# Last transform stage in sets of four banks, first weights split by row blocks, and the last sums in another order, in a kernel that mixes a long convolution with a bilinear GLU

## The chip, the cores and the metric

One core of a Trainium2 chip runs the whole kernel. The time is the device time of one execution in microseconds (us); the kernel before has a median of 628.41 us over 3 runs (627.85 to 631.08). The engines are PE (matrix products, with PEld for its weight loads), DVE (VectorE), ACT (ScalarE), POOL (GpSimd, here a queue for DMAs that add in memory) and SP (a queue for all other DMAs).

## The reference

For 2048 tokens of 512 channels the output is a gated mix of two branches, `g * a + (1 - g) * b`, with `g = sigmoid(sum(x * gate_w))` for each token.

```python
def _A_ref(u, log_A_real, A_imag, C_real, C_imag, log_dt, D_skip):
    dt = jnp.exp(log_dt)
    A = -jnp.exp(log_A_real) + 1j * A_imag
    C = (C_real + 1j * C_imag) * dt[:, None]
    P = jnp.exp((A * dt[:, None])[:, :, None] * pos[None, None, :])
    K = 2.0 * jnp.einsum("dn,dnl->dl", C, P).real
    ...                       # a causal convolution of u with K by FFTs of 2 * L points
    return y + u * D_skip[None, None, :]
def _B_ref(x, w_gate, w_up, w_down):
    g = jnp.einsum("bsd,df->bsf", x, w_gate)
    u = jnp.einsum("bsd,df->bsf", x, w_up)
    return jnp.einsum("bsf,fd->bsd", g * u, w_down)
```

F, the inner width of the GLU, is 1792, and the state has 128 numbers for each channel.

## The kernel before

**The GLU branch** works through 14 blocks of 128 inner columns (f) in five groups of 3, 2, 3, 3 and 3, and in each group through four chunks of 512 tokens. To keep float32 accuracy every operand is split into a high part (rounded to float32r by an ACT cast: `xhi`, `whi`, `dhi`, `hh`) and a low part (what is left, by a DVE subtraction: `xlo`, `wlo`, `dlo`, `hl`), and every block product of 128 rows and 512 columns is three matmuls: high x low, low x high, high x high. For one f and one chunk, `hidden` makes 12 matmuls into the bank `pg` (gate) and 12 into `pu` (up); ACT copies `pg` to `h`, DVE multiplies `pu` into it, ACT and DVE split it to `hh` and `hl`. `down` then sums all f of the group into four `y` banks, of which two exist. ACT scales a finished `y` by 1 - g into `acc`, and a DMA stores it (first group, SP) or adds it to the output in memory (later groups, POOL). These 2016 matmuls, one by one, are called products below.

**The convolution branch** is done by Fourier transforms written as small matmuls. `u_part` takes 8 sets of first transforms of the input (`k<-in,w_t` in the trace) and stores them to the memory tensor `su_d`. For each of 16 blocks of 32 channels DVE and ACT build the tables `x` and `v` of powers, and one set of matmuls (`k<-v,x`, `k_block`) makes the kernel K from them. After every fourth block the quarter q of the channels is complete: `k_first` transforms its K in two sets (`k<-kt,w1k_t`, stored to `sk_d`), `m_second` makes four sets (`w2s`), `m_product` multiplies on DVE, `m_inverse` makes two sets back (`k<-y,w3s`, stored to `y_d`), and `m_last` the last stage (`w4`): it reads `y_d` back and makes two calls for each quarter, each of two banks; ACT multiplies them by the gate g into a staging tile `ts`, which POOL adds to the output. All these sets share four banks `k`. In the last quarter the tables are read into tiles that are free by then (`late`), the mixing is on DVE, and the part for tokens 12 to 15 of each partition stays in SBUF (`late["fin"]`).

**The end.** `ends` takes the output rows of the last chunk, as far as they were summed in memory, into the tile `kt` and for each of four row blocks adds the last `y` times 1 - g (`scalar_tensor_tensor`), then `late["fin"]` for the last 128 channels, and stores the block by SP.

**The start.** `first_loads` issues the first chunk's x, and the weights of f 0, 1 and 2, into tiles that are free at first. Three warm-up matmuls on zeros (each leaves two records) run meanwhile.

**The order of the work** is planned when the program is built. Each step is added as a task with its engine, an estimate of its time, what it reads and writes, a rank and sometimes an earliest time (`after`). `Work.run` places the tasks greedily: of all that could start, the one with the earliest start, then the lowest rank. The order that comes out is then the fixed program order of each engine. A `hidden` step n may not be planned before `T_STEP * n`, with `T_STEP = 10.3`. So an edit of one task's cost or start moves much of the order behind it.

## Time and profile before

| | |
|---|---|
| median of 3 runs | 628.41 us (627.85 to 631.08) |
| the profiled execution | 627.43 us, span 625.7 us |
| PE busy | 607.1 us, 97% of the span |
| DVE, ACT, POOL busy | 513.7, 421.7, 88.8 us |
| DMA | 121.67 MB, mean 194 GB/s |

The span runs from the first to the last record of the profile; the time of the execution is 1.7 us more. The profile gives, for groups of instructions or one by one, when they ran, how long, and what ended an engine's wait before them. Matmuls overlap, so a row's length is longer than its place in the sequence: products follow one another every 0.23 us, though each row says 0.39.

### The profile page before, as it was taken

To read this page: it belongs to the slowest core of one execution; us is meant where nothing else is said; L and a number is where in the kernel's file an instruction comes from. 1 tells how busy PE (TensorE), PEld (TensorE's weight loads), DVE (VectorE), ACT (ScalarE), POOL (GpSimd) and SP (SyncE) were. 2 spreads that over 40 slices of the span, in tenths; PEclk is the share of its full clock that TensorE was granted. 3 is DMA by queue.
4 is the path that set the end of the run, shared out by engine and by line. 5 is a ranking of instruction groups with operands and counts; after the bars stand their busy time and mean duration, and the time that the engine had idled before them with its cause. 6 is when DMAs were issued, how large, how long until landed. Compare 5 with 4: busy or idle time off the path is not lost.

```text
span 625.7 us, 17973 instructions
## 1 busy us (share of the span) xinstructions
PE 607.1 (97%) x7526; PEld 468.4 (75%) x7526; DVE 513.7 (82%) x808; ACT 421.7 (67%) x951; POOL 88.8 (14%) x125
## 2 busy tenths in 40 slices
PE   8999999999999899999999999999999999999993
PEld 5676777787678678877788887868788887777871
DVE  6959999999899989999749999989999962329543
ACT  6478878886895976697658866886977563534310
POOL 0211121111022101113101111030201020121101
PEclk9999999999999999999999999999999999999998
DMA  8793745555679994877667966793997959797866
GB/s 317 215 323 100 244 120 179 169 177 152 180 170 247 230 234 116 216 213 99 136 184 197 252 214 126 220 215 100 231 237 190 252 148 270 195 266 170 186 170 118
DMA packets 102422, 121.67 MB, mean 194 GB/s; under 512 B 6596, under 2 KB 65476, under 8 KB 102084
## 3 DMA queue, kind: packets, MB, share of 16 engines
q1 hardware_dynamic: 83188, 92.46, 48.1%
q0 software_dynamic: 19008, 28.06, 25.2%
q8 instruction: 59, 0.97, 0.6%
q14 instruction: 23, 0.19, 0.1%
q10 hardware_dynamic: 144, 0.00, 0.0%
HBM read 69.37 MB, written 51.12 MB: 193 GB/s over the span
## 4 chain that ended last, share of the span: by engine, by line
PE 79%; DVE 6%; DMA 5%; issue 5%; ACT 3%; SPq 0%; ACTq 0%; DVEq 0%; POOLq 0%
PE y L100 21%; PE pu L100 20%; PE pg L100 20%; PE k L100 18%; DMA out<-acc 2%; DMA raw<-in_wts 2%; DVE v L100 1%; DMA in<-in_u 1%; DVE x L100 1%; DMA ev<-in_wts 1%; DVE h L100 1%; DVE hl L100 1%; DVE wlo L100 1%; ACT acc L100 1%; DVE xlo L100 0%
## 5 line engine op out<-in xcount | busy, mean ns | idle before, releaser
L100 POOL DMA_DIRECT2D out<-acc x60 | 53.2, 943 | 351.3 <-ACT acc L100 337.8
L100 PE MATMUL y<-dhi,hl 128*128 128x512 f32 x224 | 91.5, 408 | 2.8 <-issue 1.8
L100 PE MATMUL pg<-xhi,wlo 128*128 128x512 f32 x224 | 89.6, 400 | 2.0 <-DVE wlo L100 1.0
L100 PE MATMUL pu<-xhi,wlo 128*128 128x512 f32 x224 | 89.3, 399 | 0.0
L100 PE MATMUL pg<-xlo,whi 128*128 128x512 f32 x224 | 87.5, 391 | 1.2 <-issue 0.9
L100 PE MATMUL y<-dlo,hh 128*128 128x512 f32 x224 | 87.5, 391 | 0.0
L100 PE MATMUL y<-dhi,hh 128*128 128x512 f32 x224 | 87.4, 390 | 0.0
L100 PE MATMUL pg<-xhi,whi 128*128 128x512 f32 x224 | 87.3, 390 | 0.0
L100 PE MATMUL pu<-xlo,whi 128*128 128x512 f32 x224 | 87.3, 390 | 0.0
L100 PE MATMUL pu<-xhi,whi 128*128 128x512 f32 x224 | 87.3, 390 | 0.0
L100 DVE TENSOR_TENSOR h<-pu,h 128x512 f32<-128x512 f32 x56 | 38.6, 689 | 51.5 <-PE pu L100 42.7
L100 ACT ACTIVATE acc<-y,ngate 128x512 f32<-128x512 f32 x76 | 51.5, 693 | 29.0 <-PE y L100 20.0
L100 ACT CAST hh<-h 128x512 fp32r<-128x512 f32 x56 | 34.7, 620 | 47.0 <-DVE h L100 46.8
L100 PEld LDWEIGHTS y<-dhi,hl 128*128 128x128 f32 x224 | 42.0, 187 | 25.4 <-issue 10.4
L100 ACT COPY ts<-k 128x512 f32<-128x512 f32 (+1 forms) x116 | 49.3, 496 | 14.2 <-PE k L100 14.2
L100 PEld LDWEIGHTS pg<-xhi,wlo 128*128 128x128 f32 x224 | 42.0, 188 | 17.2 <-issue 2.3
L100 ACT COPY h<-pg 128x512 f32<-128x512 f32 x56 | 32.9, 587 | 30.5 <-PE pg L100 24.9
L100 PEld LDWEIGHTS pu<-xhi,wlo 128*128 128x128 f32 x224 | 42.0, 188 | 13.5 <-issue 4.2
L100 PEld LDWEIGHTS pg<-xlo,whi 128*128 128x128 f32 x224 | 42.1, 188 | 10.2 <-issue 1.3
L100 PEld LDWEIGHTS y<-dhi,hh 128*128 128x128 f32 x224 | 42.1, 188 | 9.3
L100 PEld LDWEIGHTS pu<-xhi,whi 128*128 128x128 f32 x224 | 42.0, 188 | 9.0
L100 PEld LDWEIGHTS pg<-xhi,whi 128*128 128x128 f32 x224 | 42.1, 188 | 8.9
(103 smaller groups left out, 1169.3 us busy)
## 6 DMA issues: line engine op xcount, KB each, us to landing
raw<-in_xT SPq DMA_DIRECT2D x60, 256.0 KB, 4.4
out<-acc POOLq DMA_DIRECT2D x60, 256.0 KB, 7.0
raw<-in_wts SPq DMA_DIRECT2D x36, 256.0 KB, 5.4
su_d<-ts POOLq DMA_DIRECT2D x32, 256.0 KB, 4.7
sk_d<-ts SPq DMA_DIRECT2D x16, 512.0 KB, 5.2
y_d<-ts SPq DMA_DIRECT2D x16, 512.0 KB, 5.3
in<-sk_d SPq DMA_DIRECT2D x12, 512.0 KB, 6.8
in<-su_d SPq DMA_DIRECT2D x12, 512.0 KB, 5.9
```

The costliest lines, as they stand in the source:

```text
L100: got = getattr(self.engine, name)(*args, **kw)
```

## The change

Four edits:

1. `m_last` takes a list of halves. For quarters 0 to 2 it is now one call of eight matmuls over all four `k` banks (`halves = (0, 1)`), with four reads of `y_d` before it, of which the fourth goes to a `y` tile; for the last quarter it stays two calls of two banks. In `k_first`, the last quarter's second half is staged in two table tiles (`ri`, `e`).
2. The weights of f 0 come in four DMAs, each with the 128 columns of gate and of up that belong to one row block kt, alternating with the four DMAs of x; the first of them is issued by ACT. `first_split` splits each piece by itself (256 columns). The first `hidden` uses the high x high matmul first and high x low last. One warm-up matmul of the three is dropped.
3. The earliest time of every `hidden` is 5.0 us earlier.
4. In `ends` the addition of `late["fin"]` comes before that of `y`.

```diff
@@ -401,12 +401,15 @@
         in_y = lambda shape: new("mid", "y", shape, bufs=2)
         in_ev = lambda shape: new("mid", "ev", shape, bufs=3)
         xsrc = lambda kt: xT[P * kt : P * kt + P, :D]
-        w0 = load_two(lambda k: ("w", 0, k), in_ev, None, False)
-        x01 = load_two(lambda k: ("x", 0, 0, k), in_y, None, False)
-        for t, k, src in ((x01, 0, xsrc(0)), (w0, 0, wts[0][:, :D]), (w0, 1, wts[0][:, D : 2 * D]), (x01, 1, xsrc(1))):
-            add("sp", 0.42, lambda t=t, k=k, src=src: sp.dma_start(t.t[:, k], src), w=[(t, k)], dma=256, rank=-1)
-        x23 = xT[2 * P : 4 * P, :D].rearrange("(k p) t -> p k t", k=2)
-        load_two(lambda k: ("x", 0, 0, 2 + k), in_y, x23)
+        w0 = raws["w0"] = in_ev([P, 2, D])
+        xt = [load_two(lambda k, n=n: ("x", 0, 0, 2 * n + k), in_y, None, False) for n in range(2)]
+        wsrc = wts[0][:, : 2 * D].rearrange("p (k d) -> p k d", k=2)
+        for kt in range(KT):
+            t, k, ks = xt[kt // 2], kt % 2, slice(P * kt, P * kt + P)
+            add("sp", 0.42, lambda t=t, k=k, kt=kt: sp.dma_start(t.t[:, k], xsrc(kt)), w=[(t, k)], dma=256, rank=-1)
+            e, q = ("sp", sp) if kt else ("act", act)
+            add(e, 0.42, lambda q=q, ks=ks: q.dma_start(w0.t[:, :, ks], wsrc[:, :, ks]), w=[(w0, ("k", kt))], dma=128, rank=-1)
         for f in (1, 2):
             load_two(lambda k, f=f: ("w", f, k), in_ev, wts[f][:, : 2 * D].rearrange("p (k d) -> p k d", k=2))
@@ -416,20 +419,35 @@
         add("dve", 0.2, lambda: dve.memset(zero.t, 0.0), w=[zero], rank=-1)
         def warm():
-            for _ in range(3):
+            for _ in range(2):
                 pe.matmul(scratch.t, zero.t[:, :P], zero.t, start=True, stop=True)
-        add("pe", 4.0, warm, r=[zero], w=[scratch], rank=-1)
+        add("pe", 3.4, warm, r=[zero], w=[scratch], rank=-1)
     def weights(fs):
         for f in fs:
             ws[f] = [new("glu", n, [P, 2 * D], F32R, len(GROUPS[0])) for n in ("whi", "wlo")]
+            if f == 0:
+                for kt in range(KT):
+                    first_split(kt)
+                    if kt + 1 < KT:
+                        tokens(0, 0, kt + 1)
+                continue
             for c in range(2):
                 load(("w", f, c), wts[f][:, c * D : (c + 1) * D])
                 split(ws[f][0], ws[f][1], c, ("w", f, c))
-            if f == 0:
-                for kt in range(1, KT):
-                    tokens(0, 0, kt)
+    def first_split(kt):
+        hi, lo, t, k = *ws[0], raws["w0"], ("k", kt)
+        cut = lambda x: x.rearrange("p (c d) -> p c d", c=2)[:, :, P * kt : P * kt + P]
+        src = lambda: t.t[:, :, P * kt : P * kt + P]
+        add("act", 0.38, lambda: act.copy(cut(hi.t), src()), r=[(t, k)], w=[(hi, k)], rank=0)
+        add(
+            "dve", 0.42,
+            lambda: dve.tensor_tensor(out=cut(lo.t), in0=src(), in1=cut(hi.t).bitcast(F32), op=ALU.subtract),
+            r=[(t, k), (hi, k)], w=[(lo, k)], rank=0,
+        )
     def down_weights(fs):
         for f in fs:
@@ -445,16 +463,19 @@
     THREE = ((1, 0), (0, 1), (0, 0))
-    def product(pg, which, w, x, kt, after):
+    def product(pg, which, w, x, kt, after, first):
         base = which * D + kt * P
+        part = ("k", kt) if first else which
+        three = THREE[::-1] if first else THREE
         def fn():
-            for n, (a, b) in enumerate(THREE):
+            for n, (a, b) in enumerate(three):
                 pe.matmul(
                     pg.t, w[a].t[:, base : base + P], x[b].t, start=kt == 0 and n == 0, stop=kt == KT - 1 and n == 2
                 )
-        add("pe", 0.681, fn, r=[(w[0], which), (w[1], which), x[0], x[1]], w=[pg], rank=2, after=after)
+        add("pe", 0.681, fn, r=[(w[0], part), (w[1], part), x[0], x[1]], w=[pg], rank=2, after=after)
     steps = []
@@ -464,14 +485,14 @@
         pg = [new("ps_g", n, [P, D]) for n in ("pg", "pu")]
         x = dict(xs)
-        after = T_STEP * len(steps)
+        after = T_STEP * len(steps) - 5.0
         steps.append(f)
         pairs = [(which, kt) for which in range(2) for kt in range(KT)]
         if f == 0:
             pairs.sort(key=lambda p: p[1])
         for which, kt in pairs:
-            product(pg[which], which, ws[f], x[kt], kt, after)
+            product(pg[which], which, ws[f], x[kt], kt, after, not steps[1:] and f == 0)
         h = new("glu", "h", [P, D])
         hh, hl = (new("glu", n, [P, D], F32R, len(GROUPS[0])) for n in ("hh", "hl"))
         add("act", 0.59, lambda: act.copy(h.t, pg[0].t), r=[pg[0]], w=[h], rank=0)
@@ -528,19 +549,19 @@
         for r, y in ending:
             t = t0 + r
             add(
+                "dve", 0.25,
+                lambda r=r: dve.tensor_tensor(
+                    out=sums.t[:, r, P * (KT - 1) :], in0=sums.t[:, r, P * (KT - 1) :], in1=late["fin"].t[:, r],
+                    op=ALU.add,
+                ),
+                r=[late["fin"]], w=[(sums, r)], rank=0,
+            )
+            add(
                 "dve", 0.69,
                 lambda r=r, t=t, y=y: dve.scalar_tensor_tensor(
                     sums.t[:, r], y.t, ngate[:, t : t + 1], sums.t[:, r], op0=ALU.mult, op1=ALU.add
                 ),
                 r=[y, (m_gate, LAST)], w=[(sums, r)], rank=0,
-            )
-            add(
-                "dve", 0.25,
-                lambda r=r: dve.tensor_tensor(
-                    out=sums.t[:, r, P * (KT - 1) :], in0=sums.t[:, r, P * (KT - 1) :], in1=late["fin"].t[:, r],
-                    op=ALU.add,
-                ),
-                r=[late["fin"]], w=[(sums, r)], rank=0.5,
             )
             add(
                 "sp", 0.42, lambda r=r, t=t: sp.dma_start(ov[:, t, :], sums.t[:, r]), r=[(sums, r)], w=[(m_out, t)],
@@ -938,7 +959,12 @@
         tt(0.19, lambda: kt.t[:, 48, :], lambda: kt.t[:, 48, :], lambda: skip[:, q], ALU.add, [m_skip], [kt])
         for h in range(2):
-            banks, sts = [bank() for _ in range(4)], [stage([P, 8, 4, 32]) for _ in range(2)]
+            banks, shape = [bank() for _ in range(4)], [P, 8, 4, 32]
+            if q == KT - 1 and h:
+                sts = [new("tab", n, shape) for n in ("ri", "e")]
+            else:
+                sts = [stage(shape) for _ in range(2)]
             def fn(h=h, banks=banks):
@@ -1113,22 +1139,27 @@
             )
-    def m_last(q, half):
-        fins = [stage([P, 8, P])]
-        if q == KT - 1 and half == LAST // 2:
-            fins = [stage([P, 4, P]) for _ in range(2)]
-            late["fin"] = fins[LAST % 2]
-        place = lambda i: (fins[0], 4 * i) if len(fins) == 1 else (fins[i], 0)
-        banks, rhs, src = [bank() for _ in range(2)], [], [m_w4]
-        for i in range(2):
-            r = 8 * half + 4 * i
+    def m_last(q, halves):
+        places = []
+        for half in halves:
+            if q == KT - 1 and half == LAST // 2:
+                fins = [stage([P, 4, P]) for _ in range(2)]
+                late["fin"] = fins[LAST % 2]
+                places += [(f, 0) for f in fins]
+            else:
+                fin = stage([P, 8, P])
+                places += [(fin, 0), (fin, 4)]
+        tokens = [8 * half + 4 * i for half in halves for i in range(2)]
+        banks, rhs, src = [bank() for _ in tokens], [], [m_w4]
+        for r in tokens:
             if q == KT - 1:
                 rhs.append(lambda h, r=r: late["y"].t[:, 16 * h + r : 16 * h + r + 4])
                 src += [late["y"]]
                 continue
-            t = inp([P, 1, 2, 4, P])
+            t = inp([P, 1, 2, 4, P]) if r < 12 else new("mid", "y", [P, 1, 2, 4, P], bufs=2)
             rhs.append(lambda h, t=t: t.t[:, 0, h])
             src += [t]
             rows_y = y_d[q].rearrange("k (h r) d -> k h r d", h=2)[:, :, r : r + 4]
@@ -1145,10 +1176,9 @@
                         tile_position=(0, 64 * h),
                     )
-        add("pe", 2.0, fn, r=src, w=banks, rank=1, hold=fins)
-        for i, f in enumerate(banks):
-            r = 8 * half + 4 * i
-            fin, n0 = place(i)
+        fins = list(dict.fromkeys(f for f, _ in places))
+        add("pe", 0.92 * len(banks), fn, r=src, w=banks, rank=1, hold=fins)
+        for f, r, (fin, n0) in zip(banks, tokens, places):
             to = lambda fin=fin, n0=n0: fin.t[:, n0 : n0 + 4]
             def mix_act(f=f, r=r, to=to):
@@ -1163,13 +1193,13 @@
             args = ("dve", 0.69, mix_dve) if q == KT - 1 else ("act", 1.14, mix_act)
-            add(*args, r=[f, (m_gate, r // 4)], w=[(fin, i)])
+            add(*args, r=[f, (m_gate, r // 4)], w=[(fin, n0)])
         cs = slice(P * q, P * q + P)
-        for k, fin in enumerate(fins):
+        for fin in fins:
             if fin is late.get("fin"):
                 continue
-            n = 8 // len(fins)
-            rs = range(8 * half + n * k, 8 * half + n * k + n)
+            rs = [r + k for r, (f, _) in zip(tokens, places) if f is fin for k in range(4)]
+            n = len(rs)
             add(
                 "pool", 0.95,
                 lambda fin=fin, rs=rs: pool_q.dma_start(ov[:, rs[0] : rs[-1] + 1, cs], fin.t, accum_op=ALU.add),
@@ -1206,8 +1236,8 @@
                     "sp", 0.42, lambda lanes=lanes: sp.dma_start(t.t[lanes], y_d[q, lanes]),
                     r=[(m_y, (q, T))], w=[(t, T)], dma=512,
                 )
-        for half in range(2):
-            m_last(q, half)
+        for halves in ((0,), (1,)) if q == KT - 1 else ((0, 1),):
+            m_last(q, halves)
     first_loads()
```

How the planned order moves is shown at three places. The first is PE at the last stage of the last quarter (`w4`), with the tile numbers of the program; before, it stands near PE's end:

```order
L100 MATMUL y_8281<-dlo_6698,hh_8111 128x512
L100 MATMUL y_8281<-dhi_6684,hh_8111 128x512
L100 MATMUL y_8281<-dhi_6691,hl_8218 128x512
L100 MATMUL y_8281<-dlo_6706,hh_8216 128x512
L100 MATMUL y_8281<-dhi_6691,hh_8216 128x512
L100 MATMUL y_8281<-dhi_6897,hl_8267 128x512
L100 MATMUL y_8281<-dlo_6899,hh_8261 128x512
L100 MATMUL y_8281<-dhi_6897,hh_8261 128x512
L100 MATMUL k_8291<-v_8116,w4_t_91 64x512 x2
L100 MATMUL k_8294<-v_8116,w4_t_91 64x512 x2
L100 MATMUL k_8298<-v_8116,w4_t_91 64x512 x2
L100 MATMUL k_8301<-v_8116,w4_t_91 64x512 x2
```

In the changed program the same set stands here on PE:

```order
L100 MATMUL y_8105<-dhi_6956,hl_8040 128x512
L100 MATMUL y_8105<-dlo_6966,hh_8035 128x512
L100 MATMUL y_8105<-dhi_6956,hh_8035 128x512
L100 MATMUL y_8105<-dhi_6971,hl_8074 128x512
L100 MATMUL y_8105<-dlo_6979,hh_8068 128x512
L100 MATMUL y_8105<-dhi_6971,hh_8068 128x512
L100 MATMUL k_8115<-v_7881,w4_t_91 64x512 x2
L100 MATMUL k_8118<-v_7881,w4_t_91 64x512 x2
L100 MATMUL k_8125<-v_7881,w4_t_91 64x512 x2
L100 MATMUL k_8128<-v_7881,w4_t_91 64x512 x2
```

Before, 9 products follow the set, the last of four `y` sums; in the changed program 138 products follow it, in which are the whole last chunk's three `hidden` steps and its four sums. Between the last `w3s` set and this one stand 48 products before and 63 now.

The second place is DVE at the end of the program, where `kt` is the tile of the last sums and `ts` the staging of the last stage. Before:

```order
L100 TENSOR_TENSOR h<-pu,h 128x512
L100 TENSOR_TENSOR hl<-h,hh 128x512
L100 SCALAR_TENSOR_TENSOR kt<-y,ngate,kt 128x512 x3
L100 TENSOR_TENSOR ts<-k,gate 128x512 x4
L100 TENSOR_TENSOR kt<-kt,ts 128x128 x3
L100 SCALAR_TENSOR_TENSOR kt<-y,ngate,kt 128x512
L100 TENSOR_TENSOR kt<-kt,ts 128x128
```

In the changed program:

```order
L100 TENSOR_TENSOR ts<-k,gate 128x512 x3
L100 TENSOR_TENSOR kt<-kt,ts 128x128 x4
L100 TENSOR_TENSOR h<-pu,h 128x512
L100 TENSOR_TENSOR hl<-h,hh 128x512
L100 TENSOR_TENSOR h<-pu,h 128x512
L100 TENSOR_TENSOR hl<-h,hh 128x512
L100 TENSOR_TENSOR h<-pu,h 128x512
L100 TENSOR_TENSOR hl<-h,hh 128x512
L100 SCALAR_TENSOR_TENSOR kt<-y,ngate,kt 128x512 x4
```

The last stage's mixing and the additions of its part now stand ahead of the last chunk's `h` and `hl`, and one `scalar_tensor_tensor` is the last instruction instead of two.

The third place is ACT at the start. Before:

```order
L100 DMA small<-in_rows 128x4
L100 ACT_TABLE_LOAD
L100 CAST xhi<-y 128x512
L100 CAST whi<-ev 128x512 x2
L100 CAST xhi<-y 128x512 x3
L100 CAST whi<-ev 128x512 x4
L100 COPY h<-pg 128x512
```

In the changed program:

```order
L100 DMA ev<-in_wts 128x2x128
L100 DMA small<-in_rows 128x4
L100 ACT_TABLE_LOAD
L100 CAST xhi<-y 128x512
L100 CAST whi<-ev 128x2x128
L100 CAST xhi<-y 128x512
L100 CAST whi<-ev 128x2x128
```

Each row block's x and weights are now cast in turn; the small DMA, which DVE's first work needs, is issued behind a weight DMA. Elsewhere the order has moved too: on PE, the products now stand in 61 unbroken stretches and before in 62, and the set of the sixteenth `k_block` stands behind 1602 products, before behind 1698.

## Rows read from the trace of the kernel before

**Rows 1.** The page's first part: busy us (share of the span) and instructions

```profile
PE 607.1 (97%) x7526; PEld 468.4 (75%) x7526; DVE 513.7 (82%) x808; ACT 421.7 (67%) x951; POOL 88.8 (14%) x125
```

**Rows 2.** Busy us (instructions) by engine in six stretches; stretch, length, engines, clock, DMA

```profile
0.00:60.00 60.00, 56.73 (x227) 39.63 (x227) 45.98 (x101) 41.53 (x105) 10.11 (x37) 1.00 0.74 244
60.00:300.00 240.00, 235.42 (x2719) 182.55 (x2718) 228.78 (x355) 188.42 (x418) 38.71 (x46) 1.00 0.69 182
80.00:515.00 435.00, 430.04 (x5929) 338.53 (x5928) 398.91 (x597) 329.61 (x749) 60.49 (x69) 1.00 0.72 186
300.00:320.00 20.00, 20.00 (x135) 15.30 (x134) 8.65 (x12) 11.36 (x27) 3.46 (x4) 1.00 0.67 162
320.00:500.00 180.00, 179.07 (x2959) 142.68 (x2958) 171.12 (x252) 135.73 (x315) 20.37 (x22) 1.00 0.78 202
617.10:625.70 8.60, 0.00 (x0) 0.00 (x0) 1.00 (x2) 0.00 (x0) 0.00 (x0) 0.68 0.99 203
```

**Rows 3.** Instructions in order, the first 14 us: start, length, engine, operation [wait before]

```profile
3.07 1.01 SPq L100 DMA_DIRECT2D ev<-in_wts  x2
...
4.67 0.62 ACT L100 CAST xhi<-y 128x512 fp32r<-128x512 f32 x1 [2.21 <-DMA y<-in_xT]
...
5.03 0.34 PEld L100 LDWEIGHTS k<-acc 128*128 128x128 f32 x1 [0.52 <-issue]
...
6.71 0.69 DVE L100 TENSOR_TENSOR wlo<-ev,whi 128x512 fp32r<-128x512 f32 x1
...
7.46 0.50 PE L100 MATMUL pg<-xhi,wlo 128*128 128x512 f32 x1 [1.02 <-DVE wlo L100]
7.57 0.19 PEld L100 LDWEIGHTS pg<-xlo,whi 128*128 128x128 f32 x1
...
8.88 0.55 DVE L100 SCALAR_TENSOR_TENSOR small<-small 128x4 f32<-128x4 f32 x3
...
13.21 0.19 PEld L100 LDWEIGHTS pg<-xhi,wlo 128*128 128x128 f32 x1 [0.42 <-ACT h L100]
```

**Rows 4.** Groups by shape, DVE and ACT: count, busy us, mean ns, idle before

```profile
L100 DVE TENSOR_TENSOR h<-pu,h 128x512 f32<-128x512 f32 x56 | 38.6, 689 | 51.5 <-PE pu L100 42.7 <-ACT h L100 5.7 <-ACT ts L100 2.5
L100 DVE TENSOR_TENSOR v<-v,sq 128x256 f32<-128x256 f32 x16 | 6.7, 421 | 3.2 <-ACT sq L100 3.2
L100 ACT COPY ts<-k 128x256 f32<-128x256 f32 x56 | 17.1, 390 | 5.0 <-PE k L100 5.0
```

**Rows 5.** Chain of waits, one last-stage set of two banks: start, us, what

```profile
280.44 1.36 PE y L100 x6
281.80 1.87 PE k L100 x8
283.67 2.99 PE y L100 x12
```

**Rows 6.** Instructions in order, the last 30 us

```profile
611.10 3.65 PE L100 MATMUL k<-v,w_t 128*64 128x512 f32 x16 [0.96 <-PE y L100]
...
614.06 2.88 POOL L100 DMA_DIRECT2D out<-ts  x2 [30.96 <-DVE ts L100]
...
615.83 4.40 SPq L100 DMA_DIRECT2D out<-kt  x4
...
616.63 0.39 PE L100 MATMUL y<-dhi,hh 128*128 128x512 f32 x1
617.05 0.75 DVE L100 SCALAR_TENSOR_TENSOR kt<-y,ngate,kt 128x512 f32<-128x512 f32 x1 [0.84 <-PE y L100]
617.84 0.29 DVE L100 TENSOR_TENSOR kt<-kt,ts 128x128 f32<-128x128 f32 x1
```

**Rows 7.** SP queue's waits from 595 to 627: us in total, times, longest

```profile
SPq L1283 <- DMA out<-ts: 3.4, 1, 3.4
```

**Rows 8.** DMAs issued from 618.6 to 618.8: count, KB each, us to landing

```profile
out<-kt SPq DMA_DIRECT2D x1, 256.0 KB, 6.1
```

**Rows 9.** DMAs issued from 132 to 140, a store by itself

```profile
out<-acc SPq DMA_DIRECT2D x1, 256.0 KB, 2.0
```

## The prediction

> **What bounds the kernel now.** I read the page's first part, then a table of stretches, then the instructions one by one at the start and at the end, where the table shows idle time. The first part says PE: 607.1 of 625.7 us busy [rows 1]. The table says where the other 18.6 us are [rows 2]: in the first 60 us PE stands still for 3.3, from 60 to 300 us for 4.6, from 320 to 500 us for 0.9, and after the last product for the whole 8.6 us to the end. The granted clock is full in all stretches up to the end. DVE is the next engine: 95.3% busy from 60 to 300 us (228.78 of 240) and 95.1% from 320 to 500 us, but only 43% from 300 to 320 us. So time can be won in four places: before the first product, in PE's turns between products and small sets, in its waits, and after its last product. Products follow one another every 0.227 us (six in 1.36 [rows 5]); their number, 2016, stays.
>
> **The change part by part.** The sum is made against the profiled execution, 627.43 us (span 625.7), which is 1.0 us below the median of 628.41; the forecast puts that 1.0 back.
>
> *The start: 0.5 us less.* Now the first product begins at 7.46, after a wait for `wlo` [rows 3]. In the new order it needs only the high parts: the `xhi` cast begins when x lands at 4.67 and takes 0.62, a 256-column piece of `whi` some 0.39 (ACT copies of that shape [rows 4]), so the first product can start at 5.75, 1.7 us earlier. But the products behind it need the low parts, and DVE makes those: per row block 0.69 for `xlo` and 0.42 for a piece of `wlo` (a 256-column subtraction [rows 4]), four times, 4.4 us. Between them the order keeps eight steps of the small chain, three of which take 0.55 [rows 3], together 1.5. From 5.3 on, less some overlap, that ends near 11.1; four products follow it, so f 0 ends near 12.0 against 7.46 + 24 x 0.227 = 12.9. The first product of f 1 then waits for its own `wlo`: four more small steps and 0.69, about 12.7, against 13.21 now (a wait for ACT's `h` [rows 3]). I take 0.5. The ends: 1.7 less, if DVE keeps up; and 1.1 more, because the weights of f 1 are now issued behind a wait for x, at 4.7 or later instead of 3.1 [rows 3]. They land no later if the queue is still full with x then, which is what 0.5 assumes.
>
> *The joined sets: 0.5 us less.* A set of two banks takes 1.87, and one of four 3.65 [rows 5, 6], so each pair saves 0.09, three pairs 0.3. Coming back from a set costs more: 12 products take 2.99 behind it instead of 2.72 [rows 5], 0.27. Six sets become three, but some stood beside other sets already; in the order PE's unbroken stretches of products go from 62 to 61, one return. Together 0.5, between 0 and 1.1. The added wait is for four reads of `y_d` instead of two before each joined set; behind it on PE are the products. Between the last `w3s` set of a quarter and the joined set the order has 117 to 147 products, 26 us at least; a write and four reads of 512 KB, each at twice the 2.0 us of a 256 KB store by itself [rows 9], are 20 us even one after another, so I cost it at nothing. ACT mixes the same four banks, in one run; it is 67% busy [rows 1].
>
> *The last set: 1.0 us less.* PE waits 0.96 us in front of it [rows 6]: the reads of `y_d` have not landed. With 63 instead of 48 products ahead of it, PE arrives 15 x 0.227 = 3.4 us later by its own work, 2.4 more than the wait. That margin covers the three x loads that SP now issues around these reads; if they cost more than it, the gain goes back to 0.
>
> *The tail: 4.5 us less.* From the start of the last product (616.63 [rows 6]) to the end are 9.07 us: 0.42 until DVE begins, 0.75 and 0.29 for its two steps, the last store issued between 618.6 and 618.8, 6.1 us until it lands [rows 8], and 0.9 behind it. POOL's two additions of the last stage are issued at 614.06 and after [rows 6], their landing is what SP waits for longest at the end, 3.4 us [rows 7], and the DMA engines are 99% busy meanwhile [rows 2]. In the new order 138 products, 31 us, stand between that set and the end, so these additions, and those of the `acc` tiles, land before the last stores begin. One DVE step is left, 0.75. The store then goes out in a nearly empty queue: one by itself took 2.0 us [rows 9]; the store before it starts 9 products, 2.0 us, ahead, so I take 2.4. New tail: 0.42 + 0.75 + 0.06 (hand-over, an estimate) + 2.4 + 0.9 = 4.5. The ends are 6.1 for the store as now, a gain of 0.8, and 2.0, a gain of 4.9. Of the 4.5, edit 4 by itself is only 0.3.
>
> *What costs nothing.* The last quarter's tables as staging, the earlier `after` and DVE's other order add no work; they act through the order. PE's waits between 60 and 500 us, 5.5 us in all, will be others in a new order. The DVE share is the cover here: in the new order the sixteenth `k_block` set comes 96 products, 21.8 us, earlier, mostly out of the lull at 300 to 320 us. DVE had 398.91 us of work in the 435 us between the first and the last of these sets [rows 2]. Without 96 products it has about 5.4 less (2.7 pairs of `h` and `hl`, and some x splits, at 0.69 [rows 4] less overlap): 393.5 in 413.2 us, 95.2%. That is the share which it holds now over 240 and over 180 us. So I take no change, between 3 less and 5 more.
>
> Sum: 0.5 + 0.5 + 1.0 + 4.5 = 6.5 us; 627.43 - 6.5 = 620.9 for an execution like the profiled one, 621.9 for the median.
>
> **The rivals.**
> *The array is still at half clock when the products begin.* Weight loads of one shape take 0.34 at 5.03 and 0.19 at 7.57 [rows 3]: the clock doubles in between, while the warm-up, six records, runs until 1.02 us before the first product [rows 3]. Now it has four records, ends earlier, and PE may stand still again before 5.75. If the clock has not risen by then, f 0's 24 products take up to 0.43 each: 5.75 + 10.3 = 16.1 instead of 12.0, 4 us lost: 625.9. For it speaks that the first products also have gaps; against it that the rise came somewhere between 5.03 and 7.57, so perhaps before 5.75. The Trainium skill says (TensorE: Matmul & The Clock Gate, "What's actually happening") that the default state is throttled and activity releases it. By that rule a shorter warm-up with a gap risks the half clock; the trace agrees that the warm-up began at the lower level, but shows no gap of this kind.
>
> *The end is not quiet.* The reads of `y_d` are late again and the four last stores hinder each other as now (6.1 us): 1.0 and 3.7 of the gain are gone, 626.6. For it: the four stores still come within 5 us. Against: now POOL's two additions run beside them [rows 6, 7], and these leave.
>
> *Slower: DVE can't follow the denser order.* The place is the stretch between the first and the sixteenth `k_block`, the mechanism that PE, in program order, waits at each `k<-v,x` set for a late table `v`. If DVE reaches only its present mean there, 91.7% (398.91 of 435), its 393.5 us need 429.1, and PE loses 15.9: 637.8. From 93.7% down the whole gain of 6.5 us is lost. For it: 95.2% over 413 us was never held without the lull. Against: it was over 240 us, with 4.6 us of PE waits.
>
> *The gains are cancelled one by one by new waits in the new order*, 6 us instead of none: 628, no change. The waits between 60 and 500 us would have to double; their sum now is 5.5 [rows 2].
>
> **How the numbers follow.** The forecast has 0.70, the clock 0.08, the unquiet end 0.08, the cancelled gain 0.04, DVE 0.10. A difference under 0.5%, 3.1 us, can't be told from no change here: the bounds are 625.3 and 631.6. The forecast's own range, 617.5 to 625, is faster; the clock half faster, half no change; the unquiet end and the cancelled gain no change; DVE slower except 0.02. So faster 0.74, same 0.18, slower 0.08. The low end, 617.5, is the forecast with the whole 1.7 at the start and 3 us less waiting; the high end, 627.5, takes in the clock and the unquiet end and leaves out most of DVE and a little below, together 0.2.
>
> **What would show it.** Right: the first product near 5.8 and f 1's near 12.7, with weight loads of 0.19; three sets of 3.65 in quarters 0 to 2; no PE wait in front of the last set, some 31 us before the last product; about 4.5 us from the start of the last product to the end of the span, with the last store landing in 2 to 3 us; PE waits of about 5 us between 60 and 500 us. Wrong: loads of 0.34 beside `pg`, waits for DVE `v` in front of `k` sets, or a last store of 5 us or more.

## The result, and the profile after

| | before | after |
|---|---|---|
| median (range), runs | 628.45 us (627.85 to 631.08), 6, on the same chip | 620.02 us (618.62 to 623.76), 6 |
| ratio, 95% interval | | 0.985 (0.982 to 0.988) |
| profiled execution / its span | 627.43 / 625.7 | 620.08 / 618.3 |
| a second set of runs, on another chip | 628.12 us | 618.63 us (616.21 to 622.82); 0.984 (0.979 to 0.990) |

The changed kernel is 8.4 us faster by the medians and 7.4 from profile to profile, where 6.5 were forecast; 620.0 stands against 621.9. The page's first part, and the table of stretches (stretch, length, busy us and instructions of PE, weight loads, DVE, ACT and POOL, granted clock, DMA share, GB/s):

```profile
PE 605.5 (98%) x7524; PEld 468.3 (76%) x7524; DVE 514.0 (83%) x810; ACT 421.1 (68%) x953; POOL 88.8 (14%) x125
```

```profile
0.00:60.00 60.00, 56.70 (x226) 39.88 (x226) 43.66 (x100) 38.47 (x96) 10.10 (x37) 1.00 0.76 243
60.00:300.00 240.00, 237.18 (x2778) 186.00 (x2778) 233.60 (x363) 193.34 (x432) 35.39 (x44) 1.00 0.67 185
300.00:480.00 180.00, 178.28 (x3069) 139.36 (x3068) 169.39 (x248) 138.68 (x332) 23.50 (x24) 1.00 0.83 208
...
609.00:618.30 9.30, 4.76 (x20) 3.30 (x18) 2.67 (x4) 0.00 (x0) 0.00 (x0) 0.94 0.30 114
```

Against [rows 1, 2]: PE's busy time shrinks by 1.6 us, its idle time by 5.8. DVE holds 97% from 60 to 300 us (233.60 of 240) and PE still stands only 2.8 us there. In the last 9.3 us the DMA engines are 30% busy; before, they were 99% busy in the 8.6 us behind the last product.

The start, instructions in order (start, length, engine, operation, wait before), to be read against [rows 3]:

```profile
4.63 0.62 ACT L100 CAST xhi<-y 128x512 fp32r<-128x512 f32 x1 [1.60 <-DMA y<-in_xT]
...
5.61 0.29 PEld L100 LDWEIGHTS pg<-xhi,whi 128*128 128x128 f32 x1 [1.94 <-ACT whi L100]
5.61 0.74 PE L100 MATMUL pg<-xhi,whi 128*128 128x512 f32 x1 [0.37 <-ACT whi L100]
...
5.96 0.38 DVE L100 TENSOR_SCALAR small<-small 128x4 f32<-128x4 f32 x2 [4.40 <-DMA small<-in_rows]
6.25 0.69 DVE L100 TENSOR_TENSOR xlo<-y,xhi 128x512 fp32r<-128x512 f32 x1
...
7.00 0.19 PEld L100 LDWEIGHTS pg<-xlo,whi 128*128 128x128 f32 x1 [1.10 <-DVE xlo L100]
...
12.70 0.19 PEld L100 LDWEIGHTS pg<-xhi,wlo 128*128 128x128 f32 x1 [0.42 <-ACT h L100]
12.70 0.50 PE L100 MATMUL pg<-xhi,wlo 128*128 128x512 f32 x1
```

The first product comes at 5.61 instead of 7.46, the second at 7.00, when DVE has made the first low part; DVE began it late because the `small` load, which stands ahead of it on DVE, landed at 5.96. From 7.00 on PE has no wait any more until the end of f 0, and f 1, which waits for ACT's copy `h` as before, begins at 12.70 instead of 13.21. The weight load of 0.29 and the next of 0.19 show the clock rising between the two products.

A joined set in the chain of waits, against the two-bank set of [rows 5]:

```profile
408.83 2.37 PE y L100 x9
411.19 3.58 PE k L100 x16
414.78 2.29 PE y L100 x9
```

The end, against [rows 6, 8]: instructions in order from 577 us, then the last store (count, KB, us to landing), then what SP waited for from 590 us (total, times, longest), against [rows 7]:

```profile
577.99 0.39 PE L100 MATMUL y<-dhi,hh 128*128 128x512 f32 x1
578.31 3.65 PE L100 MATMUL k<-v,w_t 128*64 128x512 f32 x16
...
613.54 0.39 PE L100 MATMUL y<-dhi,hh 128*128 128x512 f32 x1
613.97 0.75 DVE L100 SCALAR_TENSOR_TENSOR kt<-y,ngate,kt 128x512 f32<-128x512 f32 x1 [1.29 <-PE y L100]
```

```profile
out<-kt SPq DMA_DIRECT2D x1, 256.0 KB, 2.0
```

```profile
SPq L100 <- DVE kt L100: 36.8, 4, 32.7
SPq L1313 <- DMA out<-kt: 1.5, 1, 1.5
SPq L1313 <- PEq L1313: 0.7, 2, 0.5
```

No wait stands in front of the last set, 35 us before the last product; the last store lands in 2.0 us instead of 6.1; SP waits for no `out<-ts` any more. From the start of the last product to the end are 4.8 us (618.3 - 613.54) instead of 9.0. Before, the second of POOL's two additions, issued at 614.97, landed at 623.84, 0.9 us ahead of the last store:

```profile
out<-ts POOLq DMA_DIRECT2D x1, 256.0 KB, 8.9
```

So the 7.4 us of the profiles are: tail 4.3; start 0.5; the wait ahead of the last set 1.0; other PE waits between 14 us and the last product 0.4 (6.4 before, 6.0 after, summed over the gaps between PE's records). The rest is 1.2. By the distances from one start to the next, 0.6 of it is the joined sets and about as much lies between products that stand right behind a wait of PE, where the next one follows after about 0.4 us instead of 0.23 (ten such places before, seven after).

### The profile page after: what moved, and what is told of

Same layout as the page of the kernel before. It is cut to its first block, busy times and chain, and to the rows that moved or that the text cites. A ratio compares the mean times of both kernels' runs of the same rounds, so it can differ in the third digit from the quotient of the medians.

```text
span 618.3 us, 17975 instructions
## 1 busy us (share of the span) xinstructions
PE 605.5 (98%) x7524; PEld 468.3 (76%) x7524; DVE 514.0 (83%) x810; ACT 421.1 (68%) x953; POOL 88.8 (14%) x125
## 4 chain that ended last, share of the span: by engine, by line
PE 80%; DVE 6%; issue 6%; DMA 3%; ACT 3%; POOL 0%; ACTq 0%; DVEq 0%; POOLq 0%
PE pg L100 21%; PE y L100 21%; PE pu L100 21%; PE k L100 17%; DVE x L100 2%; DMA raw<-in_xT 1%; DMA out<-acc 1%; DVE v L100 1%; DMA small<-in_rows 1%; DVE xlo L100 1%; DVE y L100 1%; ACT e L100 1%; DVE hl L100 1%; ACT L100 0%; DVE h L100 0%
## 5 line engine op out<-in xcount | busy, mean ns | idle before, releaser
L100 ACT COPY ts<-k 128x512 f32<-128x512 f32 (+1 forms) x112 | 47.6, 496 | 10.0 <-PE k L100 9.9
L100 DVE TENSOR_TENSOR xlo<-raw,xhi 128x512 fp32r<-128x512 f32 x60 | 40.6, 687 | 12.7 <-ACT xhi L100 12.7
L100 ACT CAST xhi<-raw 128x512 fp32r<-128x512 f32 x60 | 36.7, 621 | 19.8 <-DMA raw<-in_xT 15.4
L100 PEld LDWEIGHTS pg<-xlo,whi 128*128 128x128 f32 x224 | 42.1, 188 | 10.6 <-DVE xlo L100 2.4
```

The lines of the kernel that those rows point to most:

```text
L100: got = getattr(self.engine, name)(*args, **kw)
```

## The experiments

"First f 1" is the start of the first product of f 1, "tail" the time from the start of the last product to the end of the span, "waits" the sum of PE's gaps over 0.15 us between 14 us and the last product, "gap" and "behind" the products that the order has between the last `w3s` set and the last `w4` set, and behind the latter. All of the table comes from the order and the profiles, but for the last column (median; ratio to before on the same chip, 95% interval). The recorded texts do not number the edits alike: by the list of the change, no_sets undoes edit 1 (its text says 2), no_start undoes edit 2 (its text says 1), and the "kernel with edit 1 alone" of warm3 is only_start, edit 2.

| kernel | first f 1 | gap / behind | wait ahead of last set | waits | tail | result |
|---|---|---|---|---|---|---|
| before | 13.21 | 48 / 9 | 0.96 | 7.3 | 9.0 | 628.45 |
| after | 12.70 | 63 / 138 | 0 | 6.0 | 4.8 | 620.0; 0.985 (0.982-0.988) |
| only_sets | 13.26 | 63 / 51 | 0 | 7.8 | 4.4 | 623.6; 0.991 (0.988-0.994) |
| only_start | 13.90 | 51 / 105 | 2.45 | 11.4 | 5.1 | 627.6; 1.000 (0.996-1.003) |
| only_step | 13.25 | 51 / 114 | 1.50 | 6.5 | 4.5 | 622.7; 0.990 (0.988-0.993) |
| only_sums | 13.16 | 39 / 18 | 3.23 | 13.6 | 4.2 | 632.7; 1.005 (1.003-1.008) |
| no_add | 13.29 | 48 / 9 | 0.57 | 8.9 | 4.5 | 624.7; 0.992 (0.989-0.995) |
| no_sets | 12.60 | 51 / 114 | 1.35 | 12.5 | 4.5 | 630.5; 1.001 (0.999-1.004) |
| no_start | 13.34 | 63 / 42 | 0 | 6.7 | 4.1 | 622.8; 0.991 (0.988-0.994) |
| late10 | 11.69 | 63 / 42 | 0 | 7.6 | 4.8 | 621.4; 0.987 (0.984-0.990) |
| warm1 | 14.36 | 63 / 138 | 0 | 6.7 | 4.8 | 622.6, one run |
| warm3 | 12.62 | 63 / 138 | 0 | 6.6 | 4.8 | 620.6; 0.988 (0.985-0.991) |
| after_again | 12.56 | 63 / 138 | 0 | 4.8 | 4.8 | 618.6; 0.984 (0.979-0.990) |
| light_acc | 14.19 | 63 / 138 | 0 | 2.4 | 4.8 | 617.8; 0.983 (0.979-0.986) |

**Each edit by itself.** Four kernels add one edit each to the kernel before. Of each some lines are shown; in only_sums the whole `add` of these lines also moves ahead of that of `y`.

```diff
# only_sets: the joined sets alone
-    def m_last(q, half):
+    def m_last(q, halves):
...
-        add("pe", 2.0, fn, r=src, w=banks, rank=1, hold=fins)
+        add("pe", 0.92 * len(banks), fn, r=src, w=banks, rank=1, hold=fins)
```

> Edit 1 alone on the kernel before (joined sets, the last quarter's second half of k_first staged in table tiles). In its order 51 products follow the last set (9 before, 138 in the changed kernel), and 63 stand between the last w3s set and it. Theory A, most of the gain comes from the last set leaving the end: 51 products are 11.6 us, enough for POOL's two additions to land, so the tail from the start of the last product is 4.8 us as in the changed kernel (9.07 before), PE waits 0 in front of the set, and with 0.5 to 1.2 us from fewer returns the time is 622 us. Rival B, the joined sets win by fewer returns of PE from small sets and the tail is tied to other edits: 626 to 627.5 us.

```diff
# only_start: the first weights by blocks of rows, two warm-up products
-            for _ in range(3):
+            for _ in range(2):
...
+            if f == 0:
+                for kt in range(KT):
+                    first_split(kt)
```

> Edit 2 alone (first weights in four pieces, high parts first, two warm-up matmuls). The order of the sets is not edited, but 105 products now follow the last set (9 before), 51 stand between the last w3s set and it. Theory A, the place of the last set decides: tail 4.8 us instead of 9.07, start 0.5 less, PE's wait in front of the last set about 0.3 instead of 0.96: 623 us. Rival C, the edit wins only what it does at the start, 0.5 us: 628 us.

```diff
# only_step
-        after = T_STEP * len(steps)
+        after = T_STEP * len(steps) - 5.0
```

> Edit 3 alone (the earliest planned time of each hidden step 5.0 us earlier; one number). 114 products follow the last set, 51 stand between the last w3s set and it. Theory A: tail 4.8 us, 623.5 us, with no change in what any engine computes. Rival D, the number matters only together with the other edits: 628 us.

```diff
# only_sums: the last sums' steps in the other order
-                r=[late["fin"]], w=[(sums, r)], rank=0.5,
+                r=[late["fin"]], w=[(sums, r)], rank=0,
```

> Edit 4 alone (the addition of the last stage's part before that of y). 18 products follow the last set (9 before), but only 39 stand between the last w3s set and it (48 before), so PE waits 2.0 us longer for the reads, about 3 us, and has 2.0 us less behind it. Theory A: DVE's last step is 0.3 us shorter and POOL's additions still run beside the last stores: between 627.5 and 629 us, no change. Rival E, the order of the last sums is what shortens the tail: 624 us.

Two came as expected (623.6 and 622.7 us), two did not: only_start gained nothing (its 627.6 is Rival C's number, but not its mechanism: the tail is short and the start late) and only_sums, where only the long wait ahead of the last set came as expected, lost 3 us against the 629.46 of before on its chip. The tail is short in all four, and in each the last set has moved away from the end, also where a single number was changed: the plan places it, and any of the edits moves the plan. What differs is the middle. In only_start the clock rose only at 10.1 us, so f 1 began at 13.90; PE waited 2.75 us for `hl` at 32.7, with the granted clock at half for 3.4 us behind it, and 2.45 us for `v<-y_d` ahead of the last set; in only_sums the last set has only 39 products between itself and the last `w3s` set, PE waits 3.23 us ahead of it, and the granted clock is at half from 612.7 to 619.5 and from 623.0 to 626.4 us. The tail of 4.2 us is no gain there: POOL's additions still ran beside the first two of the last stores, which took 4.9 and 5.5 us, and the last two, of 2.2 and 2.1 us, were short only because the last products came so late (the last one began at 627.8, and the second addition landed at 628.1).

**The additions by themselves.** The kernel before without the last quarter's two accumulating stores.

```diff
-            if fin is late.get("fin"):
+            if q == KT - 1:
                 continue
```

> The kernel before, but the last quarter's two accumulating stores of POOL are left out, so the last block of channels is not added for the rows that they carry. The order on PE is that of before: the last `w4` set 9 products before the end, 0.96 us of wait ahead of it. Theory A (these two transfers are what the last stores share the end with): tail near 5 instead of 9.0, 624.4 us. Rival (the four stores of 256 KB within 5 us hinder each other): the last store still takes 5 to 6 us, 627.5 to 628.5 us.

624.65 us, as Theory A had it, and with the order of before: 9 products behind the last set, two DVE steps, four stores within 3 us. Its last product, DVE's last steps and its four last stores (count, KB, median us to landing):

```profile
618.38 0.40 PE L100 MATMUL y<-dhi,hh 128*128 128x512 f32 x1
618.81 0.75 DVE L100 SCALAR_TENSOR_TENSOR kt<-y,ngate,kt 128x512 f32<-128x512 f32 x1 [0.86 <-PE y L100]
619.60 0.29 DVE L100 TENSOR_TENSOR kt<-kt,ts 128x128 f32<-128x128 f32 x1
```

```profile
out<-kt SPq DMA_DIRECT2D x4, 256.0 KB, 2.2
```

The four stores land in 2.0 to 2.5 us, the last, issued at 619.92, in 2.0, where it took 6.1 [rows 8]. So it was the two additions that made the end long, not the stores that hindered each other, and the second DVE step cost nothing that shows. The run takes away the sharing and the additions' own landing (623.84 of 625.7 in before) together, so how much of the 4.5 us is which is not shown; but since the second addition itself landed only 0.9 us ahead of the last store, quicker stores alone could not have won much more than that.

**One edit undone.** no_sets is the changed kernel with sets of two banks again, no_start with the old start (the hunks above, the other way round).

> The changed kernel with edit 2 undone: sets of two banks again in quarters 0 to 2; the last `w4` set stands 114 products before the end and 51 behind the last `w3s` set. Theory A (joining saves returns and in-set time, about 1.2 us, and the gap of 63 products saves the wait ahead of the last set): tail 4.5 to 5.2, up to 1.5 us of wait ahead of the last set, 621.5 to 623 us. Rival (joining is worth nothing by itself, only the shifted order is): 620 us.

> The changed kernel with edit 1 undone (first weights by halves of columns again, three warm-up products); the last `w4` set stands 42 products before the end and 63 behind the last `w3s` set. Theory A (the start is worth 0.5 us and the rest adds up): f 1's first product at 13.2, tail 4.2 to 5.2, no wait ahead of the last set, 620.5 to 621.5 us. Rival (the waits of another middle weigh more than the start): more than 9 us of waits between 14 us and the last product, 623 us or more.

Both are slower than the changed kernel by more than Theory A had it: no_start 622.75 (1.2 us above the 621.5 that it allowed at most, 4.1 above the changed kernel on the same chip), no_sets 630.5, which neither theory expected. In the profile of no_start, of the slowest of its six runs (625.5), f 1 (13.34) and the tail (4.1) are within 0.2 us of what was expected and the waits are not the 9 us of the rival, but at two of them, of 2.19 and 2.60 us, the granted clock falls, to half for 10.2 us together. In the profile of no_sets the tail is right and the wait ahead of the last set is 1.35 us, where the two other kernels with a gap of 51 products have 1.50 and 2.45; but PE stands still for 12.5 us in all. Against the profile of the changed kernel (spans 628.2 and 618.3) the waits are 6.5 us more, the sets 0.6; two stretches at half clock add an estimated 1.6 each (eight products at 0.43 us where fifteen would have run at 0.23), and tail and start take off 0.4: 9.9 of the 9.9 us. The largest wait, in order, by the DMA queues and by stretches:

```profile
314.28 0.81 PE L100 MATMUL k<-v,x 128*32 128x64 f32 x38
319.56 0.81 PE L100 MATMUL k<-v,x 128*32 128x64 f32 x24 [4.46 <-issue]
320.30 0.80 PE L100 MATMUL y<-dhi,hl 128*128 128x512 f32 x1
```

From 315.1 to 317.2 us (queue, kind: packets, MB, share of 16 engines):

```profile
q1 hardware_dynamic: 893, 0.45, 76.7%
q0 software_dynamic: 72, 0.11, 29.8%
```

From 317.2 to 318.4 us:

```profile
q1 hardware_dynamic: 742, 0.37, 108.0%
q8 instruction: 1, 0.02, 5.3%
q0 software_dynamic: 5, 0.01, 4.6%
```

```profile
315.10:319.50 4.40, 0.00 (x0) 0.00 (x0) 0.46 (x2) 1.88 (x8) 0.00 (x0) 1.00 1.12 277
319.93:323.34 3.41, 3.41 (x21) 2.66 (x13) 2.94 (x3) 0.69 (x1) 0.38 (x1) 0.50 0.28 77
323.40:326.80 3.40, 3.40 (x16) 2.81 (x15) 2.10 (x3) 2.73 (x12) 0.41 (x1) 1.00 0.57 77
```

PE stops in the middle of a `k` set, after 104 of its 128 small matmuls, and nothing that the profile shows holds it ("issue"). DVE and ACT then wait for PE. A packet of the instruction queue q8 comes at 317.30, 2.2 us after PE has stopped, lands at 318.31, and PE goes on 1.24 us later. Then the granted clock is at its lower level for 3.41 us. There are 59 such packets of 16 KB in every kernel here:

```profile
q8 instruction: 59, 0.97, 0.6%
```

59 packets for the 15,048 matmuls and weight loads of PE (7524 of each in the changed kernel's page) are 255 each, so q8 is taken to be PE's own queue. Of the other waits of the profiles, a part ends in the same way, 1.2 to 1.6 us after such a packet has landed: 2.7 us in all in before, 3.9 in after, 8.7 in no_sets. Their places say the same: counted in PE's matmuls, the four of after stand before number 1757, 2520, 5443 and 6713, and the distances, 763, 2923 and 1270, are within two of 6, 23 and 10 times 127, that is, of whole blocks of 254 matmuls and loads. The Trainium skill says (Runtime: NRT & Kernel Launch, "Instruction fetch mechanics") that an engine's instructions are streamed in blocks of 16 KiB, 256 instructions, and that the cost of passing from one to the next is mostly hidden. The trace agrees on the size, and not on the second point behind sets of small matmuls.

**What else can be had at the start.** late10 keeps DVE's small chain out of the first ten microseconds of the plan; warm1 and warm3 change the warm-up, with the order as it is.

```diff
# late10
-        def exp(us, src, er, en, ep, ei, r, w):
+        def exp(us, src, er, en, ep, ei, r, w, after=0.0):
...
-                add("dve", us * share, go, r=r, w=w, rank=1)
+                add("dve", us * share, go, r=r, w=w, rank=1, after=after)
...
-        exp(0.15, part(0), part(1), part(2), part(3), part(4), [], [m_small])
+        exp(0.15, part(0), part(1), part(2), part(3), part(4), [], [m_small], 10.0)
# warm1 (warm3: range(3))
-            for _ in range(2):
+            for _ in range(1):
```

> The changed kernel with one number more: DVE's small chain, the first instructions that the changed kernel puts ahead of and between the `xlo` and `wlo` of f 0, may not be placed before the tenth microsecond of the plan, so no low part stands behind the wait for the `small` load (until 5.96 us in the changed kernel). The plan behind it shifts as well: the last `w4` set stands 42 products before the end instead of 138, 63 products behind the last `w3s` set as in the changed kernel. Theory A (start, return and tail add up; any place of the last set far from both the end and the `w3s` set will do): f 1's first product near 11.4 instead of 12.70, the tail still 4.2 to 5.2, no wait ahead of the last set: 618.8 us. Rival (the waits of the new middle decide, as in the kernels with single edits, where waits of 2 to 3 us were followed by stretches at half clock): f 1 at 11.4 as well, but 3 to 6 us of new waits, 621 to 624 us.

> The changed kernel with one warm-up product instead of two; the order is the same, and PE stands still longer before the first real product at 5.6 us. Theory A (the first 24 products wait for DVE's low parts anyway, so the clock matters little): f 1's first product at 12.7 to 13, 620 to 621 us. Rival (the warm-up is what raises the clock before the products begin): the clock rises near 10 us or later, first products of 0.43 us, f 1 at 13.9 or later, 621.5 us or more.

> The changed kernel with a third warm-up product; the order is the same. With one warm-up the clock rose at 10.97 us instead of 6.15 and f 1's first product came at 14.36 instead of 12.70. Theory A (with two the clock is up in time): f 1 at 12.7 again, the warm-up now ends about 6.5, 619.5 to 621 us. Rival (in some executions two are not enough, as in the kernel with edit 1 alone, whose clock rose at 10.14): median 1 us lower and a narrower spread, 618.5 to 619.5 us.

In late10 DVE begins the first `xlo` at 5.14 instead of 6.25, no wait for it is left on PE, and f 1 begins at 11.69, 1.0 us earlier than in the changed kernel. But the plan behind it is another one, which has a wait of 2.13 us for ACT's `h` at 104.5, followed by 3.4 us at half clock; the time, 621.4, lies in the rival's range (on another chip than the changed kernel's; the ratios, 0.987 and 0.985, do not differ clearly). In warm1 the clock rose at 10.97 and f 1 began at 14.36; in warm3 it rose at 5.61 and f 1 began at 12.62. The time of warm3, 620.6, cannot be told from that of the changed kernel. Neither beats it.

**The same kernel again, and with less traffic.** after_again is the changed kernel, unchanged. In light_acc POOL's stores `out<-acc` carry an eighth of their bytes.

```diff
-                "pool", 0.95, lambda: pool_q.dma_start(ov[:, t, :], acc.t, accum_op=ALU.add),
+                "pool", 0.95, lambda: pool_q.dma_start(ov[:16, t, :], acc.t[:16], accum_op=ALU.add),
```

> The changed kernel once more, not a character changed, for a second profile of it. In the profile of the changed kernel 3.9 us of PE's waits end 1.4 to 1.5 us after a 16 KB packet of PE's own instruction queue has landed (waits before 213.53, 254.01, 448.91 and 535.92); with one warm-up product less and the same order such waits stood at other places, one of 3.38 us. Theory A (these blocks of instructions come late by chance, with what else the DMA engines carry): tail 4.8 and first products as before, waits of this kind at other places and between 2 and 6 us in all, 618.5 to 624 us. Rival (the order fixes them): the same waits at the same four products, 620 us.

> The changed kernel with the same order and the same instructions, but POOL's accumulating stores `out<-acc` carry 16 of the 128 partitions (16 KB... 32 KB instead of 256 KB), so most of what they should add to the output is left out: about 13 MB less traffic. Theory A (PE's blocks of instructions come late because the DMA engines are full): waits behind such a block under 1.5 us in all instead of 3.9, no stretch at half clock, tail the same, 616 to 618 us. Rival (PE runs through the small products faster than a block can follow, whatever the traffic): 3 to 4 us of these waits remain, 619 to 620.5 us.

In after_again two of the four waits of the instruction queue are there again, smaller (0.68 before 212.62 and 0.25 before 252.24), two are gone, and a new one of 2.43 us stands before 538.14:

```profile
534.74 0.97 PE L100 MATMUL k<-y,w3s 32*64 32x128 f32 x47
538.14 0.47 PE L100 MATMUL k<-y,w3s 32*64 32x128 f32 x12 [2.43 <-issue]
538.53 0.80 PE L100 MATMUL pg<-xhi,wlo 128*128 128x512 f32 x1
539.12 0.63 PE L100 MATMUL pg<-xlo,whi 128*128 128x512 f32 x1
539.55 0.63 PE L100 MATMUL pg<-xhi,whi 128*128 128x512 f32 x1
```

So neither theory holds whole: the order fixes where a wait can stand (the new one is 127 matmuls behind the one at 535.93 that is gone, the next block), and which of these places are late, and by how much, changes from one execution to the next. The products behind the wait follow one another at 0.43 us instead of 0.23; that goes on for 3.4 us and costs an estimated 1.6.

In light_acc the same order has 1.0 us of such waits (0.86 and 0.15), where after, after_again and warm3 have 3.9, 3.4 and 5.1. PE's busy time from 60 to 600 us, of after and of light_acc:

```profile
60.00:600.00 540.00, 535.00 (x7241) 417.64 (x7241) 464.72 (x705) 380.80 (x856) 78.66 (x88) 1.00 0.77 196
```

```profile
60.00:600.00 540.00, 538.47 (x7260) 421.02 (x7259) 467.08 (x708) 382.83 (x866) 73.63 (x88) 1.00 0.63 171
```

That speaks for Theory A, in one profile. The times do not show it: 617.84 us lies in the range of Theory A, but also within the spread of after_again. One reason stands in the same profile, at its start, where the program is that of after:

```profile
7.62 0.63 PE L100 MATMUL pg<-xhi,wlo 128*128 128x512 f32 x1
8.05 0.63 PE L100 MATMUL pu<-xhi,whi 128*128 128x512 f32 x1
8.47 0.63 PE L100 MATMUL pu<-xlo,whi 128*128 128x512 f32 x1
...
10.18 0.57 PE L100 MATMUL pg<-xhi,wlo 128*128 128x512 f32 x1
10.59 0.39 PE L100 MATMUL pu<-xhi,whi 128*128 128x512 f32 x1
```

The clock came up only near 10.5 us, and f 1 began at 14.19 instead of 12.56 to 12.70, 1.5 to 1.6 us later.

## Why the prediction was right, point by point

*The start, 0.5 us: right in size, partly by luck.* First product forecast at 5.75, measured 5.61; f 1 at 12.7, measured 12.70. But the chain in between was another. In the sum DVE's low parts hold the products until 11.1, and f 1 waits for its own `wlo`. In the trace only the first `xlo` holds PE, until 7.00; DVE then keeps ahead, the other products follow at PE's own pace, the last at 12.31, and f 1 waits for ACT's `h` (0.42 in its row above). That first `xlo` was late for a reason that the sum did not have: the head of DVE's queue waits for `small` until 5.96. late10 shows that this wait and the small steps were worth 1.0 us.

*The clock rival: its mechanism is real, its size was not 4 us.* In the profiles of after, after_again and no_sets the clock was up at 6.15, 6.03 and 5.91 us. In only_start and light_acc, which have the same two warm-up products and the same split weights, it came at 10.1 and 10.6. That cost 1.2 to 1.6 us at f 1, not 4, since the clock rose within f 0 and only some eight of the 24 products ran at 0.43 us. So this start has it in some executions and not in others; three warm-up products are not shown to be faster. The rule of the Trainium skill that the forecast weighed here (TensorE: Matmul & The Clock Gate, "What's actually happening": throttled by default, released by activity) agrees with warm1, where the clock came up last, at 10.97, and warm3, where it came up first, at 5.61, each in one profile.

*The joined sets, 0.5 us: right, 0.6 measured.* In the trace of before all six two-bank sets are followed by a product that starts 0.52 us behind the last set instruction instead of 0.23, and in that of after only three are; but most of the three returns that are gone is spent inside the joined sets. From its first instruction to the next product a two-bank set takes 1.34 + 0.52 us, a joined one 3.06 + 0.52: 0.14 less than two, 0.4 for three. One step from a product to a set is gone as well (0.32 instead of 0.23), and one second product behind a return (0.34): 0.2 more. The forecast's caution was sound too: two of the six sets stood directly behind `k<-v,x` sets, which now return to products themselves. Undoing the edit cost far more than that (10 us by the medians), through the order: by the account above 9.3 of the 9.9 us between the profiles are waits, half clock and the two ends.

*The wait ahead of the last set, 1.0 us: right.* The margin was the gap of 63 products. In the eight profiles with 63 there is no such wait; with 39 to 51 there are 0.57 to 3.23 us.

*The tail, 4.5 us: right.* 4.8 us were left, 4.5 forecast, and a gain of 4.3 instead of 4.5. no_add shows the cause that the sum named, POOL's two additions, in the old order, and rules out that the four stores hinder each other. Two terms were off and nearly cancel: the last store took 2.0 us instead of 2.4, and from its landing to the end were 1.6 us (616.75 to 618.3) instead of 0.9. Edit 4, counted as 0.3, shows no gain in it: no_add, without it, has a tail of 4.5.

*The waits in the middle, 0 (3 less to 5 more): right in the changed kernel* (0.4 less), and the range was needed: over the kernels above the waits go from 4.8 to 13.6 us (2.4 in light_acc). This term, which I left at zero, differs by more from kernel to kernel than the start, the joined sets and the wait ahead of the last set were worth together (2.0 us). *The DVE rival* did not occur: DVE held 97% over 240 us, and in the profiles of after and after_again no `k<-v,x` set waits at all. *The cancelled gain* is what happened to only_start, only_sums and no_sets, whose new waits ate a tail gain of 4 us and more. It had 0.04; after it had happened to three of the six kernels with other combinations of these edits, that looks low.

The number came a little better than forecast, 620.0 against 621.9 (7.4 us from profile to profile against 6.5). The 0.9 us between the last two are 0.4 less waiting in the middle and about 0.6 in the products behind the waits, with 0.1 more in the sets and 0.2 less in the tail. Neither of the first two is in the sum, and both could as well have gone the other way.

What stays open: why a block of instructions comes late at one place and not at another. In no_sets the DMA engines were full at the time; at 535.7 us in after_again they were not. light_acc suggests, in one profile, that POOL's traffic has a part in it; no run separates queues from bandwidth.

## What to carry to other kernels

A transfer that is off the critical path for the whole kernel can still be what the last store shares the end with: look at who else lands in the last 10 us, and move that work by one stage rather than trim the last steps. When a planner sets the order, any edit, one number included, deals the waits in the middle anew, and here they weigh as much as the edits; judge an edit by the term that it was made for as well as by the time, and run it with its neighbours undone. Count what a joined or removed set saves from its first instruction to the next product, start to start, in both traces: the return is longer than a product, but the length of the set's row already holds a part of it.

## What the runs showed of the hardware

A set of some hundred small matmuls on PE, about 15 ns apart, can run ahead of its own instructions: PE then stood still for 0.15 to 4.46 us with nothing waited for, until 1.2 to 1.6 us after a 16 KB packet of its instruction queue had landed, at places that lie whole multiples of about 127 matmuls apart.

Longer waits of PE can cost twice: at twelve waits of 1.89 to 4.46 us, none of them at the start, the granted clock fell to the lower of its two levels, 1.2 instead of 2.4 GHz, for 3.4 us (6.8 at two of them), and products came every 0.43 us instead of 0.23. At waits of 2.10 (only_sets), 2.19 (only_sums) and 2.45 us (ahead of the last set of only_start) it did not.

The last 256 KB store of the end took 6.1 us with two accumulating stores of POOL beside it and 2.0 without them; four such stores issued within 2.4 us, without the accumulating ones, took 2.0 to 2.5 each.
